# A fused attention and feed-forward kernel: gates on later loads removed, plan times of DMA transposes changed, two more x tiles transposed by TensorE

## The chip, the cores and the metric

The kernel runs on one core of a Trainium2 chip. Its time is the device time of one execution in microseconds (us). Four executions of the kernel before took 213.44 to 215.19 us, with a median of 213.62 us. One execution was recorded by the hardware profiler; it took 213.64 us.

## The reference

The program computes attention and feeds its result to a two-layer network. Cut to what matters (batch 4, 8 heads, 768 positions, head dimension 64; 3072 tokens, model width 512, hidden width 2048):

```python
scores = scale * q @ k.T + bias            # bias: -slope[h] * distance
keep = is_global | is_local                # first 8 positions, or the last 96
scores = where(keep, scores, -1e9)
a = softmax(scores)
x = (a @ v).transpose(0, 2, 1, 3).reshape(3072, 512)
h = x @ w_in
out = (relu(h) ** 2) @ w_out
```

Inputs and output are float32 in DRAM. The kernel computes with bfloat16 operands and sums in float32.

## The kernel before

**Tiles.** The 3072 tokens are 24 tiles of 128 (index `j`, six to a sequence). For the attention of a tile only its own keys and those of the tile to its left matter; the eight global keys are copied into the left tile's columns. The feed-forward part takes two tiles at a time, so there are 12 blocks. Each block has 8 steps of the first product (`s1`, line 689: 8 matmuls of 256 columns into `hT`), each followed by a relu on ScalarE (ACT, line 710), a square on VectorE (DVE, line 722) and one step of the second product (`s2`, line 759: 4 matmuls of 512 columns into `acc`). A finished block is copied from PSUM and stored to DRAM from SyncE's queue (SP, line 794).

**Path of one tile.** GpSimd (POOL) issues three loads that cast to bfloat16, line 200: q and k into a buffer `qk_ring[slot(j)]`, and v into a buffer of its own. Tiles 0 to 5 have a buffer each; tiles from 6 on share three buffers in turn, so load `j` must wait until tile `j-3` has been transposed out of its buffer. q and k are then transposed to `qkT[j % 12]`: for tiles below `JQK = 6` by TensorE through PSUM (`tr`, line 383) with a copy; from tile 6 on by one DMA transpose that SyncE issues (`T`, line 407). Then come the scores (`sc`, line 463), the exponential (line 509), the multiplication by the bias factors (line 534), the product with v (`pv`, line 576) and the normalization (lines 603 and 604), which gives `x` of the tile. `x` is transposed to `xT` for the feed-forward part: for tiles below `JX = 6` by TensorE (`trx`, line 639) with a copy on DVE or ACT (lines 317 and 315); from tile 6 on by a DMA transpose that SyncE issues (line 663).

**Gates.** From tile 8 on, a load has a gate: a memset of the first column of `qk_ring[slot(j)]` on DVE (line 357, 60 ns). It overwrites what the transpose of tile `j-3` reads and is itself overwritten by the load, so the load follows the gate, and the gate follows the transpose. The place of the gate in DVE's order sets the time from which the load may go:

```python
deps=qk_users[slot(j)] + [ld, xT_sp.get(j - 3)], key=base - 9,
```

Here `ld` is the data of load `j-1`, and `xT_sp` holds the DMA transposes of x (only those).

**The planner.** The order of instructions on each engine is written by `Plan`, a list scheduler that runs when the program is built. Each operation has a cost per engine (made-up times such as 0.87 us for an `s1` step), a list of operations that must come before it, and a key. Time after time the planner takes the operation with the smallest start plus 0.01 times its key. While an engine has a choice of work, the start is the same for all, and the key decides. Operations that emit nothing stand for time that passes: `("data", j)` for the landing of a load, `("moved", j)` and `("xmoved", j)` for the landing of a DMA transpose, `("land", ...)` for the first loads. They occupy pretended resources, `DMAQ` or `DMA`. The plan sets order alone; on the chip every instruction waits for the data it needs, and each engine and each queue runs in the order written.

A tile's keys are counted from `base = 8*(j//2) - lead + 4*(j%2)`, with a lead of 12 (10 and 11 for tiles 6 and 7), on the scale on which `s1` step `n` has the key `n` (plus constants by kind of operation, in `SHIFT`). Scores of tile `j` also depend, in the plan, on `s1` step `4*j - 12`. The DMA transpose of tile `j` depends, in the plan, on x of tile `j-3` having been transposed (`xT_op[j - 3]`). `s1` of a block depends on the `xT` of both its tiles.

Of the kernel before, what the change touches and what calls it, by code (L numbers as in the profile page):

```python
# [104 lines left out]
def kernel(  # L105
# [17 lines left out]
    NT = B * TPB  # L123
# [17 lines left out]
    NFIRST = 4  # L141
    NSPLIT = 4
    NBIAS = 3
    JQK, JX = 6, 6
    NQ, NKT = 3, 2 * TPB
    NG = 8 - NACC
    G = ("g", NG)
# [27 lines left out]
    pbt = const([P, 2, P], FP32, "pbt")  # L175
    pbw = const([P, 2, P], FP32, "pbw")
    plan = Plan()
    LEADS = {6: 10, 7: 11}
    NHS = 14
    NWARM = 8  # L180
    NLATE, NO = 2, 4
# [9 lines left out]
    def slot(j):  # L191

        return j if j < NFIRST + 2 else NFIRST + 2 + j % NQ
# [34 lines left out]
    def load_tile(j):  # L228
        load_part(0, j)
        load_part(1, j)  # L230
        load_v(j)
# [81 lines left out]
    def any_copy(e, dst, src):  # L313
        if e == "ACT":
            nc.scalar.copy(dst, src)  # L315
        else:
            nc.vector.tensor_copy(dst, src)
# [25 lines left out]
    for j in range(NT):  # L343
        b, t = divmod(j, TPB)
        first = t == 0
        need = 8 * (j // 2)
        base = need - LEADS.get(j, LEAD) + 4 * (j % 2)


        if j in late:  # L350
            def emit_load(e, j=j):
                load_tile(j)
            gate = None
            if j >= NFIRST + 2 + NQ - 1:

                def emit_gate(e, j=j):
                    nc.vector.memset(qk_ring[slot(j)][:, :, :1], 0.0)  # L357

                gate = plan.op(
                    ("gate", j), {"DVE": 0.07}, emit_gate, deps=qk_users[slot(j)] + [ld, xT_sp.get(j - 3)],  # L360
                    key=base - 9,
                )
            ld = plan.op(
                ("load", j), {"POOLQ": 2.6}, emit_load,
                deps=qk_users[slot(j)] + [ones[j], gate], key=base, ready=issue[0],
            )
            qk_users[slot(j)] = []
            ld = plan.op(("data", j), {"DMAQ": 2.7}, None, deps=[ld])
            land["q", j] = land["k", j] = land["v", j] = ld
# [6 lines left out]
        for n in range(2) if j < JQK else ():  # L376
            users = []

            def emit_tr(e, j=j, n=n, fp=fp):
# [11 lines left out]
                deps=[land["qk"[n], j]], key=base, takes=(*G, [users]),  # L391
            )

            def emit_T(e, j=j, n=n, T_=T_):
                any_copy(e, T_[:, n], tiles.pop(("tr", n, j)))

            c = plan.op(
                ("T", n, j), {"DVE": 0.61 if fp else 0.41, "ACT": 0.48}, emit_T,
                deps=[tr] + ku, key=base + 0.1,
            )  # L400
# [4 lines left out]
        if j >= JQK:  # L405
            def emit_dT(e, j=j, T_=T_):
                nc.sync.dma_start_transpose(
                    out=T_.rearrange("p n a c -> p (n a) c"),
                    in_=qk_ring[slot(j)].rearrange("p n c -> p (n c)"),
                )  # L410

            T = plan.op(
                ("T", j), {"SP": 1.3}, emit_dT,
                deps=[land["q", j], land["k", j], xT_op[j - 3]] + ku, key=base - 6,
            )
            T = plan.op(("moved", j), {"DMAQ": 1.2}, None, deps=[T])
            qk_users[slot(j)].append(T)
            parts = [T]
        kT_users[j % NKT] = ku = []

# [51 lines left out]
        deps = list(parts)  # L472
# [26 lines left out]
        for g in range(groups):  # L499
            for odd in range(2):  # L500
# [26 lines left out]
                def emit_mul(e, j=j, odd=odd, g=g, first=first):  # L527
# [11 lines left out]
                    deps=[x_, maskE0[odd] if first else None],  # L539
# [23 lines left out]
        for hf in range(2):  # L563
# [22 lines left out]
            deps = [mul[0, g], mul[1, g], land["v", j]]  # L586
# [11 lines left out]
            def emit_norm(e, j=j, hf=hf):  # L598
# [14 lines left out]
                deps=[p_] + norm, key=base + 2.3 + 2 * hf,  # L613
# [18 lines left out]
        if j < JX:  # L632
            users = []

            def emit_f(e, j=j):
                trx = ps_g.tile([P, KM, P], BF16, name="trx", tag="g")
                x = tiles["x", j].rearrange("p h d -> p (h d)")
                for kt in range(KM):
                    nc.tensor.transpose(
                        out=trx[:, kt, :], in_=x[:, kt * P : (kt + 1) * P], identity=ident  # L640
                    )
                tiles["trx", j] = trx

            f_ = plan.op(
                ("trx", j), {"PE": 0.24}, emit_f, deps=norm, key=base + 5,
                takes=(*G, [users]),
            )

            def emit_xT(e, j=j, blk=blk, tt=tt):
                if tt == 0:  # L650
                    tiles["xT", blk] = work.tile([P, KM, 2 * P], BF16, name="xT", tag="xT", bufs=3)
                any_copy(
                    e, tiles["xT", blk][:, :, tt * P : (tt + 1) * P], tiles.pop(("trx", j))
                )

            c = plan.op(("xT", j), {"DVE": 0.41, "ACT": 0.48}, emit_xT, deps=[f_], key=base + 5.1, takes=xT_ring)
            users += [f_, c]
            xusers.append(f_)
        else:
            def emit_xT(e, j=j, blk=blk, tt=tt):  # L660
                if tt == 0:
                    tiles["xT", blk] = work.tile([P, KM, 2 * P], BF16, name="xT", tag="xT", bufs=3)
                nc.sync.dma_start_transpose(
                    out=tiles["xT", blk][:, :, tt * P : (tt + 1) * P],
                    in_=tiles["x", j].rearrange("p h d -> p (h d)"),
                )

            c = plan.op(("xT", j), {"SP": 1.2}, emit_xT, deps=norm, key=base + 5, takes=xT_ring)
            xop = xT_sp[j] = c
            c = plan.op(("xmoved", j), {"DMAQ": 0.9}, None, deps=[c])  # L670
            xusers.append(c)
        xT_op[j] = c
        xT_users.append(c)
        xT_of[blk] = xT_users
# [7 lines left out]
    for n, (blk, s) in enumerate(order1):  # L682
        users = []

        def emit_s1(e, blk=blk, s=s):
# [15 lines left out]
            deps=[xT_op[2 * blk], xT_op[2 * blk + 1], land["win", s]],  # L701
# [28 lines left out]
    for o in plan.ops:  # L730
        if o["name"][0] == "sc":
            j = o["name"][1]
# [4 lines left out]
    for blk in range(NBLK):  # L737
# [9 lines left out]
        for s, sub, half in order2:  # L747
# [5 lines left out]
            def emit_s2(e, blk=blk, s=s, sub=sub, half=half, w=w, cols=cols, own=own):  # L753
# [17 lines left out]
                deps=[d, land["wout", s]] + users[-1:],  # L771
# [5 lines left out]
            if s == NSTEP - 1:  # L777
                ousers = []

                def emit_o(e, blk=blk, sub=sub, half=half, cols=cols):  # L780
# [6 lines left out]
                    emit_o, deps=[o], key=8 * blk + s + 1.0, takes=("o", NO, [ousers]),  # L787
# [4 lines left out]
                def emit_st(e, blk=blk, sub=sub, half=half, cols=cols):  # L792
# [9 lines left out]
                    deps=[ev, s1_ops[NLATE, 0] if blk < NLATE - 2 else None],  # L802
# [43 lines left out]
```

## Time and profile before

| What | Value |
|---|---|
| median of four runs | 213.62 us |
| profiled execution | 213.64 us |
| its span, first to last instruction | 211.9 us |
| TensorE matmul busy | 202.4 us (96%) |
| VectorE busy | 138.9 us (66%) |
| ScalarE busy | 119.9 us (57%) |
| GpSimd busy | 73.8 us (35%) |
| mean granted TensorE clock | 1.000 |
| DMA transposes of q and k, of x | 18 and 18 |
| gates on DVE | 16, of 60 ns each |

How to read it: busy time is the union of an engine's instructions, and since matmuls overlap in TensorE's pipeline, a high share alone says little. The page cuts the span into 40 slices and gives a digit for each (9 means 90% or more). A row of the timeline gives start, duration, engine, line, operation and tiles, and in brackets the idle time of the engine before it with what ended it. "SPq" is SyncE's queue of DMA issues; its duration is that of the issue, and the landing of the data is counted apart. "issue" is waiting that the profile explains by nothing else.

### The profile page before, as it was taken

The page shows a single profiled execution, that of the slowest core. Times are in us where ns is not written, and L with a number is a line of the kernel's source. Part 1 is how long each engine was busy: PE and PEld are TensorE (multiplying, and loading weights), DVE is VectorE, ACT ScalarE, POOL GpSimd, SP SyncE. Part 2 cuts the span into 40 slices and gives each one's busy share as a digit, 9 for nine tenths or more (in the row PEclk, how much of TensorE's full clock was granted, in tenths as well). Part 3 has the DMA queues.
Part 4 walks back from the last instruction along what each step waited for, and adds up shares of the span by engine and source line. Part 5 has one row for each costly group of instructions (what it writes and reads, how often), then busy time and mean ns, then how long its engine had stood idle before and what let it go on. Part 6 is the DMA issues. An engine that isn't in the chain of part 4 may idle for free.

```text
span 211.9 us, 4984 instructions
## 1 busy us (share of the span) xinstructions
PE 202.4 (96%) x1946; PEld 140.7 (66%) x1976; DVE 138.9 (66%) x377; ACT 119.9 (57%) x223; POOL 73.8 (35%) x91
## 2 busy tenths in 40 slices
PE   7799999999999999989999999999999999999994
PEld 3576877555766767656666666766667667666773
DVE  7589878623966866656677677575677577564530
ACT  6787668224663763843844854753845754733531
POOL 8996766440224314404404404404134400000000
PEclk9999999999999999999999999999999999999999
DMA  8999999999699999699999599998999894210202
GB/s 122 153 173 186 184 191 198 176 191 149 173 97 97 206 103 125 138 139 103 150 169 95 107 178 99 116 186 96 167 138 101 114 179 83 90 33 3 99 2 99
DMA packets 113703, 27.59 MB, mean 130 GB/s; under 512 B 104336, under 2 KB 110736, under 8 KB 113680
## 3 DMA queue, kind: packets, MB, share of 16 engines
q0 software_dynamic: 79200, 13.37, 82.4%
q1 hardware_dynamic: 34480, 13.90, 32.8%
q8 instruction: 15, 0.25, 0.5%
q14 instruction: 8, 0.07, 0.1%
HBM read 27.26 MB, written 6.29 MB: 158 GB/s over the span
## 4 chain that ended last, share of the span: by engine, by line
PE 82%; DMA 7%; POOL 5%; ACT 2%; issue 2%; DVE 0%; SPq 0%; POOLq 0%; ACTq 0%
PE hT L689 37%; PE acc L759 36%; PE sc L463 4%; PE po L576 4%; DMA win<-in_moe_w_in_dram 4%; DMA qkT<-qk 3%; POOL qk L200 3%; POOL v L200 2%; POOL win L200 1%; ACT esc L509 1%; ACT hr L710 1%; ACT o L315 0%; PE tr L383 0%; DVE hs L722 0%; POOL pbi L254 0%
## 5 line engine op out<-in xcount | busy, mean ns | idle before, releaser
L689 PE MATMUL hT<-xT,win 128*128 128x256 bf16 x768 | 98.4, 273 | 0.7 <-DMA win<-in_moe_w_in_dram 0.3
L710 ACT ACTIVATE hr<-hT 128x512 f32<-128x512 f32 x96 | 57.7, 601 | 72.1 <-PE hT L689 68.4
L759 PE MATMUL acc<-wout,hs 128*128 128x512 bf16 (+1 forms) x370 | 93.3, 370 | 2.0 <-issue 0.8
L689 PEld LDWEIGHTS <-win 128*128 128x128 bf16 x768 | 74.0, 98 | 25.5 <-DMA win<-in_moe_w_in_dram 1.1
L722 DVE TENSOR_TENSOR hs<-hr 128x512 bf16<-128x512 f32 x96 | 65.8, 688 | 32.5 <-ACT hr L710 31.5
L200 POOL DMA_DIRECT2D qk<-in_q_dram x23 | 20.6, 896 | 89.4 <-DVE qk L357 55.3
L759 PEld LDWEIGHTS <-hs 128*128 128x128 bf16 x400 | 35.7, 97 | 23.7
L509 ACT ACTIVATE esc<-sc 128x512 bf16<-128x512 f32 x78 | 43.6, 607 | 4.2 <-PE sc L463 4.0
L534 DVE TENSOR_TENSOR at<-esc,E 128x512 bf16<-128x512 bf16 x78 | 32.2, 422 | 10.9 <-ACT esc L509 9.5
L200 POOL DMA_DIRECT2D v<-in_v_dram x24 | 21.7, 904 | 1.4 <-DMA win<-in_moe_w_in_dram 0.9
L604 DVE TENSOR_TENSOR x<-po,rs 128x256 bf16<-128x256 f32 x48 | 20.4, 424 | 1.7
L200 POOL DMA_DIRECT2D qk<-in_k_dram x23 | 20.4, 887 | 1.0 <-DMA win<-in_moe_w_in_dram 0.9
L576 PEld LDWEIGHTS <-at 128*128 128x128 bf16 x352 | 16.0, 98 | 4.7 <-ACT at L509 0.8
L576 PE MATMUL po<-v,at 128*128 128x65 bf16 x352 | 17.8, 193 | 0.6 <-DMA v<-in_v_dram 0.5
L315 ACT COPY o<-acc 128x512 f32<-128x512 f32 (+1 forms) x21 | 11.2, 568 | 7.6 <-PE acc L759 7.6
L463 PEld LDWEIGHTS <-qkT 64*128 64x128 bf16 x352 | 10.0, 94 | 8.0 <-issue 4.0
L603 DVE RECIPROCAL rs<-po 128x4 f32<-128x4 f32 x48 | 8.7, 181 | 9.3 <-PE po L576 9.2
L463 PE MATMUL sc<-qkT 64*128 64x128 bf16 x192 | 13.4, 219 | 0.8 <-DMA qkT<-qk 0.6
L463 PE MATMUL sc<-qkT,qkT 64*128 64x128 bf16 x160 | 11.5, 216 | 0.0
L200 POOL DMA_DIRECT2D win<-in_moe_w_in_dram x8 | 6.2, 800 | 1.8 <-DMA win<-in_moe_w_in_dram 1.3
L200 POOL DMA_DIRECT2D wout<-in_moe_w_out_dram x8 | 5.7, 718 | 2.0 <-DMA win<-in_moe_w_in_dram 1.2
L550 DVE COPY qkT<-qkT 128x32 bf16<-128x32 bf16 x16 | 3.5, 219 | 4.4 <-PE sc L463 4.4
(41 smaller groups left out, 58.3 us busy)
## 6 DMA issues: line engine op xcount, KB each, us to landing
out_dram<-o SPq DMA_DIRECT2D x23, 256.0 KB, 2.3
v<-in_v_dram POOLq DMA_DIRECT2D x24, 128.0 KB, 5.8
qk<-in_q_dram POOLq DMA_DIRECT2D x23, 128.0 KB, 4.7
qk<-in_k_dram POOLq DMA_DIRECT2D x23, 128.0 KB, 5.2
win<-in_moe_w_in_dram POOLq DMA_DIRECT2D x8, 256.0 KB, 8.2
wout<-in_moe_w_out_dram POOLq DMA_DIRECT2D x8, 256.0 KB, 9.3
qkT<-qk SPq DMA_TRANSPOSE x18, 3.6
xT<-x SPq DMA_TRANSPOSE x18, 3.5
```

Of the source, the lines that this page charges most:

```text
L200: nc.gpsimd.dma_start(out=dst, in_=src)
L315: nc.scalar.copy(dst, src)
L463: nc.tensor.matmul(out=tiles["sc", j, odd, g][:, at, :], lhsT=qkT[(j - kt) % NKT][half, 1, pair, :], rhs=qkT[j % NKT][half, 0, pair, :], s ...
L509: nc.scalar.activation(out=esc, in_=tiles.pop(("sc", j, odd, g)).rearrange("p a c -> p (a c)"), func=Act.Exp, scale=scale,)
L534: nc.vector.tensor_mul(at, tiles.pop(("esc", j, odd, g)), bias)
L576: nc.tensor.matmul(out=po[:, hi, :], lhsT=tiles["at", j, odd, g][:, at * P : (at + 1) * P], rhs=v_sb[kj][:, h, :], start=(i == 0), stop=(i ...
L603: nc.vector.reciprocal(rs, po[:, :, D : D + 1])
L604: nc.vector.tensor_tensor(out=x[:, 4 * hf : 4 * hf + 4, :], in0=po[:, :, :D], in1=rs.to_broadcast([P, 4, D]), op=Alu.mult,)
L689: nc.tensor.matmul(out=hT[:, c, :], lhsT=w_in_sb[s][:, kt, c * P : (c + 1) * P], rhs=tiles["xT", blk][:, kt, :], start=(kt == 0), stop=(kt ...
L710: nc.scalar.activation(hr, tiles.pop(("hT", blk, s)), Act.Relu)
L722: nc.vector.tensor_mul(hs, hr, hr)
L759: nc.tensor.matmul(out=tiles["acc", blk, sub, half], lhsT=hs[:, c, sub * P : (sub + 1) * P], rhs=w_out_sb[s][:, c, cols], start=(s == 0 an ...
```

## The change

Five edits, all in what the planner is given:

- `JX` goes from 6 to 8, so x of tiles 6 and 7 is transposed by TensorE and copied, and no longer by a DMA transpose.
- Tiles 10 to 23 get a lead of 14 where they had 12.
- Tiles 6 to 11 get an operation `("seen", j)` after `("moved", j)`, which emits nothing and takes 1.6 us in the plan. The scores of the tile wait for it in the plan; the release of the buffer does not.
- Tiles 9 and 11 get the like for x, `("xseen", j)`, of 1.5 us.
- Only loads 8, 9 and 10 keep a gate (`JGATE = 11`). Later loads wait for the transpose that frees their buffer and for nothing else.

```diff
-    JQK, JX = 6, 6
+    JQK, JX = 6, 8
...
-    LEADS = {6: 10, 7: 11}
+    LEADS = {6: 10, 7: 11} | {j: 14 for j in range(10, NT)}
+    SAFE = {j: 1.6 for j in range(6, 12)}
+    SAFEX = {9: 1.5, 11: 1.5}
+    JGATE = 11
...
             gate = None
-            if j >= NFIRST + 2 + NQ - 1:
+            if NFIRST + 2 + NQ - 1 <= j < JGATE:
...
             T = plan.op(("moved", j), {"DMAQ": 1.2}, None, deps=[T])
             qk_users[slot(j)].append(T)
+            if j in SAFE:
+
+                T = plan.op(("seen", j), {"DMA": SAFE[j]}, None, deps=[T])
             parts = [T]
...
             c = plan.op(("xmoved", j), {"DMAQ": 0.9}, None, deps=[c])
             xusers.append(c)
+            if j in SAFEX:
+                c = plan.op(("xseen", j), {"DMA": SAFEX[j]}, None, deps=[c])
```

## The prediction

> **What bounds the kernel.** I read the page's slices and busy times first, then stretches of the span, then who waits for whom on TensorE, then the transposes and the queues that carry them.
>
> ```profile
> PE   7799999999999999989999999999999999999994
> PEclk9999999999999999999999999999999999999999
> DMA  8999999999699999699999599998999894210202
> ```
>
> TensorE (PE) is full in nearly every slice at full granted clock; so are the DMA engines until slice 34. Either could be the bound. The answer by stretches (columns: window, its length, then busy time and instructions of PE, weight loads, DVE, ACT, POOL) tells which:
>
> ```profile
> 22.00:43.00 21.00, 20.84 (x214) 15.55 (x215) 16.34 (x37) 12.89 (x24) 12.80 (x16) 1.00 1.66 187
> 43.00:64.00 21.00, 20.64 (x187) 13.15 (x189) 12.46 (x32) 10.42 (x20) 5.27 (x6) 1.00 1.33 150
> 64.00:85.00 21.00, 20.84 (x211) 14.57 (x214) 14.84 (x41) 10.66 (x20) 7.89 (x9) 1.00 1.32 136
> 85.00:100.00 15.00, 14.12 (x126) 9.56 (x123) 9.31 (x23) 8.51 (x16) 5.27 (x6) 1.00 1.06 125
> 100.00:203.00 103.00, 101.63 (x952) 70.80 (x969) 67.73 (x166) 59.07 (x108) 23.68 (x27) 1.00 0.97 114
> ```
>
> From 22 to 203 us PE is busy 20.84 + 20.64 + 20.84 + 14.12 + 101.63 = 178.07 of 181.00 us. The idle 2.93 us is all that any change to loads and transposes in this stretch can give back. Before 22 us the first weights arrive (tiles 0 to 5, which the diff leaves alone); after 203 us PE runs the last 40 second-product matmuls without a stop. The waits of PE in that stretch:
>
> ```profile
> PE acc L759 <- issue: 0.8, 5, 0.2
> PE sc L463 <- DMA qkT<-qk: 0.6, 1, 0.6
> PE acc L759 <- DVE qkT L550: 0.2, 1, 0.2
> ```
>
> One wait on a DMA, 0.6 us, once. The "issue" rows are short turns around score matmuls, which stay. Where the 0.6 us is, the timelines of SyncE and GpSimd show:
>
> ```profile
> 86.41 1.14 SPq L794 DMA_DIRECT2D out_dram<-o  x2
> 87.66 1.29 SPq L407 DMA_TRANSPOSE qkT<-qk  x1
> 91.74 1.19 SPq L663 DMA_TRANSPOSE xT<-x  x1
> ...
> 86.98 0.88 POOL L200 DMA_DIRECT2D qk<-in_q_dram  x1 [4.62 <-DVE qk L357]
> 87.85 0.88 POOL L200 DMA_DIRECT2D qk<-in_k_dram  x1
> 88.72 0.90 POOL L200 DMA_DIRECT2D v<-in_v_dram  x1
> ...
> 93.82 0.40 PE L463 MATMUL sc<-qkT 64*128 64x128 bf16 x8 [0.62 <-DMA qkT<-qk]
> ```
>
> The q/k transpose of tile 12 starts at 87.66, in the middle of two stores and the load of tile 13, and lands at 93.77, 6.1 us later; scores 12 start at 93.82. The landing times of the two kinds of transposes (qkT, then xT; minimum, median, maximum):
>
> ```profile
> DMA to landing us min/median/max: 3.0/3.6/6.8
> DMA to landing us min/median/max: 2.4/3.5/7.0
> ```
>
> So a transpose costs 2.4 to 3.1 us in clear queues and up to 7.0 in full ones. I paired each with its consumer's first weight load. Slack is tiny in half of the places: scores 12, 14, 16, 18 and 22 start 0.04, 0.31, 0.31, 0.31 and 0.29 us after their transpose lands; feed-forward blocks 3, 4, 7 and 8 start 0.10, 0.11, 0.04 and 0.21 us after their second xT. The old order sits on an edge, but pays only about 0.9 us there: 0.62 at scores 12 and 0.28 of weight-load wait at 129.32.
>
> **The change, part by part.**
>
> *x of tiles 6 and 7 by TensorE.* Two DMA transposes (2 x 1.19 us of SyncE) go; 8 transposes and two copies come. The rows for tiles 0 to 5:
>
> ```profile
> L639 PE MATMUL trx<-ident,x x24: 219/219/229, 11.7 to 41.9; 128*128 128x128 bf16 x24
> L317 DVE COPY xT<-trx x2: 405/415/425, 12.3 to 42.1; 128x512 bf16<-128x512 bf16 x2
> ```
>
> 219 ns is the time of one by itself; they overlap, and the group of four at 41.71 takes 0.39 us in the timeline, which is 219 + 3 x 56 ns. So 8 x 0.056 = 0.45 us of PE, all on the bound. The copies (0.42 us on DVE, or 0.59 on ACT by the row for ACT) lie beside PE: DVE is busy 12.46 of 21 us in 43 to 64. Were that cover gone, block 3 would start up to 0.6 us later. In exchange its x no longer waits for the 5.95 us transpose issued at 59.37, landed at 65.31, which made the plan fill with second-product matmuls until 65.42. Filling loses no PE time, so this earns at most 0.1 us. Bounds of this part: 0 to +0.6; I take +0.45.
>
> The Trainium skill, "TensorE: Matmul & The Clock Gate", Part 4, gives some 275 ns per 128x128 transpose in a kernel and speaks against this edit: by its figure 8 x 0.275 = 2.2 us, an estimate, and the sum would be some 1.75 us higher. The pitch of 56 ns in this trace decides against it.
>
> *Gates.* DVE loses 13 memsets of 60 ns (tiles 11 to 23): 0.8 us, off the path. More important is what they held: each load of tile j waited for its gate's place in DVE's order, 9 to 16 us after the transpose of tile j-3 freed its buffer (transpose 10 landed at 74.29, load 13 went at 86.98). Now GpSimd waits for that landing itself; nothing else is behind it but later loads. Gates 9 and 10 also lose their tie to x transposes of tiles 6 and 7 (`xT_sp` has none), so load 9 could go at about 53, when load 8 has landed (52.51), not at 56.92, and the later ones follow. From load 11 on a load can come that much earlier. Its q/k transpose can go right after the x transpose of tile j-3 instead of behind the load. Scores 12 then have microseconds of slack: minus 0.62.
>
> What it may cost: loads 10 to 13 now come nearly back to back, and transposes fly among them. The dearest transposes seen are 6.8 and 7.0 us, against 3.6 in the median. Bounds for a transpose in the new crowd: 2.4 to 7.0 us; I take 4.7, which transposes 16, 18 and 22 took, each started 0.16 us behind a load.
>
> The Trainium skill, "DMA: Bandwidth & Descriptors", Rules for kernel authors, says that a transpose next to ordinary DMAs needs nothing; that is about correct data. In time this trace disagrees (3.0 against 4.7 to 6.8 us). By that rule the old gates protected nothing and the crowd is free.
>
> *Two steps more lead for tiles 10 to 23.* Scores of tile j now follow first-product step 4j-10 (scores 12 come after step 38); by the keys they can follow step 4j-12, where the code's own dependency stands. A step lasts (192.72 - 97.22) / 48 = 1.99 us, so scores, norms and x transposes come up to 4.0 us earlier against the blocks that read them. That covers the 0.28 at 129.32 and another 3 us of lateness. The work is the same: 0 by itself.
>
> *Extra time in the plan for transposes 6 to 11 and x 9 and 11.* No instruction; it moves consumers back in PE's order where the plan expected the data too early, up to 1.6 us in plan, with other matmuls ahead of them. 0 as long as the second product has a backlog; if not, up to 1.6 us once.
>
> **Sum**, against the profiled execution (213.64 us: span 211.9 and 1.74 around it; the median of the runs is 213.62, the same): 213.64 - 0.62 - 0.28 + 0.45 = 213.2 us.
>
> **Rivals.**
>
> *The lead asks for data that are not there (214.2).* Scores 10 would move from 76.94 to 72.9, but transpose 10 started at 71.20. If its load comes no earlier than now (k landed at 69.90), a crowded transpose lands at 74.6 to 76.7. The added plan time should order other work there; an error of about 1 us remains, and x of tile 9, with 0.11 us of slack and no new lead, may land in 7.0 instead of 5.66 us: 1.2 us. One of them: about 1 us, 213.2 + 1.0 = 214.2. For it: slack was zero there before. Against: the stretch is short.
>
> *Slower: odd x transposes run into free loads, block after block (216.9).* The gate is what kept loads off certain transposes. If each x transpose of tiles 11, 13, ... 21 took the worst 7.0 us, the lateness beyond today's slack would be 1.5, 2.4, 2.0, 2.2, 2.4 and 2.2 us (today's landings 3.4, 2.4, 5.0, 4.6, 3.2 and 3.3; slacks 2.1, 2.2, 0.0, 0.2, 1.4 and 1.5). A lead gained of 2.4 us or more swallows it; at 1.5 us the losses are 0 + 0.9 + 0.5 + 0.7 + 0.9 + 0.7 = 3.7: 216.9. So it decides where less than 2.4 of the 4.0 us arrive. For it: with DMA busy, x transposes 12 and 7 took 7.0 and 5.95 beside loads. Against: a load now starts when a q/k transpose lands, some 5 us after an x transpose, and should be over before the next one 6 to 10 us later.
>
> *Much faster (211.2).* All 2.93 us of idle time vanish: 213.64 - 2.93 + 0.45. Against: most of it is turns at score matmuls, which stay.
>
> **Chances and range.** Forecast 213.2: 0.58. The early lead, 214.2: 0.20. Crowded x transposes, 216.9 (215.5 to 220): 0.18. Much faster: 0.04. About 1% (2.1 us) is what a measurement of this kernel can tell from no change; the first two lie within it, so faster 0.04, same 0.78, slower 0.18. Range: from 212.4 (half of the remaining idle time gone too) to 216.5, which leaves out 0.04 and some 0.12 of the slower case.
>
> **What would show it.** In the changed profile: PE's waits on qkT gone from 85 us on; landings of qkT with slack of 4 us or more; GpSimd's waits on DVE gone after load 10, replaced by waits on qkT; 32 trx matmuls; PE busy about 0.45 us more; median landing of both transposes above 3.6. Wrong would be: PE waiting for xT at block starts 5 to 10, or PE idle above 2.9 us between 22 and 203.

## The result and the profile after

The changed kernel takes 212.78 us (median of 34 executions, 212.23 to 214.54), the kernel before 214.37 us (median of 55, 212.84 to 218.19). The ratio is 0.9939, with a 95% interval of 0.9925 to 0.9954: about 1.3 us or 0.6% faster. Medians here are of all executions; ratios and their intervals leave out those more than 1.5% above the fastest of their kernel. The change also narrows the spread: in two later sets of runs, with 12 executions each, it stayed between 212.38 and 214.00, while the kernel before beside it went from 212.86 to 219.09.

The profiled execution took 213.1 us with a span of 211.3. The slices of TensorE, its clock and the DMA engines after:

```profile
PE   7999999999999989999999999999999999999993
PEclk9999999999999999999999999999999999999999
DMA  9999999999999999999999999999943121120202
```

The DMA digits now fall at slice 30, not 34: the loads are over about four slices earlier. By stretches (window, length, then busy time and instructions of PE, weight loads, DVE, ACT, POOL):

```profile
22.00:43.00 21.00, 20.84 (x212) 15.23 (x213) 16.09 (x36) 12.76 (x24) 11.91 (x15) 1.00 1.66 187
43.00:64.00 21.00, 20.84 (x179) 12.87 (x181) 11.36 (x31) 10.69 (x21) 10.53 (x12) 1.00 1.60 168
64.00:85.00 21.00, 20.07 (x218) 14.49 (x220) 15.58 (x39) 11.88 (x24) 9.46 (x11) 1.00 1.62 143
85.00:100.00 15.00, 14.73 (x143) 10.14 (x145) 11.17 (x26) 9.07 (x18) 3.69 (x5) 1.00 1.58 159
100.00:203.00 103.00, 101.62 (x934) 70.84 (x951) 69.27 (x156) 54.48 (x101) 18.41 (x21) 1.00 0.81 101
```

GpSimd's work (the last busy column) moves forward: 10.53 us in 43 to 64, where it was 5.27. The waits of TensorE from 22 to 203 us:

```profile
PE acc L767 <- issue: 0.6, 4, 0.2
PE sc L469 <- DMA qkT<-qk: 0.6, 1, 0.6
PE acc L767 <- DVE qkT L556: 0.3, 2, 0.2
```

The wait on qkT is no longer at scores 12. The transpose of tile 12 now starts 10.7 us earlier (it was 87.66), and its scores come when they are due:

```profile
76.93 1.25 SPq L410 DMA_TRANSPOSE qkT<-qk  x1
...
89.22 0.39 PE L469 MATMUL sc<-qkT 64*128 64x128 bf16 x7
```

It has moved to scores 10. The timelines of GpSimd, SyncE and TensorE there:

```profile
56.89 0.88 POOL L203 DMA_DIRECT2D qk<-in_q_dram  x1 [0.40 <-issue]
60.94 0.88 POOL L203 DMA_DIRECT2D qk<-in_q_dram  x1 [1.42 <-DVE qk L360]
...
68.90 5.91 SPq L410 DMA_TRANSPOSE qkT<-qk  x2
...
77.37 0.23 PE L469 MATMUL sc<-qkT 64*128 64x128 bf16 x2 [0.61 <-DMA qkT<-qk]
```

The load at 56.89 is that of tile 11, and the one at 60.94, which still waits for a gate, that of tile 10: the planner put the ungated load ahead of the gated one. Both transposes start at 68.90 and 70.74 in a full queue, and number 10 takes 8.4 us. All landings of transposes after (q/k, then x):

```profile
DMA to landing us min/median/max: 3.1/5.6/8.4
DMA to landing us min/median/max: 2.4/3.4/6.7
```

So a q/k transpose became 2 us dearer in the median (3.6 to 5.6), and from scores 11 on it does not matter, because there is slack enough (3.17 us or more). Slack is the time from the landing of a transpose to its consumer's first weight load, paired as in the prediction:

| Consumer | slack before, us | slack after, us |
|---|---|---|
| scores 9, 10 | 0.14, 2.66 | 4.38, 0.04 |
| scores 12, 14, 16, 18, 22 | 0.04, 0.31, 0.31, 0.31, 0.29 | 8.19, 5.02, 10.28, 10.57, 13.05 |
| scores 13, 15, 17 | 3.85, 4.70, 3.36 | 3.17, 9.12, 12.26 |
| feed-forward block 4 | 0.11 | 2.92 |
| blocks 5, 6, 7, 8 | 2.10, 2.18, 0.04, 0.21 | 1.53, 4.90, 4.62, 2.93 |

Scores of tile j follow first-product step 4j-12 from tile 11 on (step 36 for tile 12, 40 for 13, 44 for 14), as the lead of 14 lets them (steps are counted from 0). What holds the loads now is the transpose that frees their buffer, with the gates left over for loads 8 to 10 alone (GpSimd's waits after):

```profile
POOL qk L203 <- DMA qkT<-qk: 52.2, 10, 9.9
POOL qk L203 <- DVE qk L360: 13.2, 3, 6.8
```

**Two profiles with every record.** Both profiles above lack some 30 of TensorE's matmuls (1946 and 1953 in the page's first part, where 1976 and 1984 were issued). Later profiles of the same two kernels have them all. The stretch from 22 to 203 us, before and after:

```profile
22.00:203.00 181.00, 180.01 (x1706) 123.29 (x1705) 120.90 (x297) 102.06 (x187) 54.46 (x64) 1.00 1.15 130
```

```profile
22.00:203.00 181.00, 181.00 (x1712) 123.81 (x1711) 123.77 (x287) 99.33 (x184) 53.93 (x63) 1.00 1.18 129
```

In that execution of the changed kernel TensorE is busy for 181.00 of 181.00 us. In that of the kernel before the 0.99 us that is missing is exactly two waits on transposes, at scores 12 and at block 3:

```profile
PE sc L463 <- DMA qkT<-qk: 0.7, 1, 0.7
PE hT L689 <- DMA xT<-x: 0.3, 1, 0.3
```

No "issue" rows are left in either. By this comparison some two of the 2.93 us that the first profile called idle were matmuls that had not been recorded.

### The profile page after: what moved, and what is told of

Read it like the earlier page. It is cut to its first block, busy times and chain, and to the rows that moved or that the text cites. A ratio compares the mean times of both kernels' runs of the same rounds, so it can differ in the third digit from the quotient of the medians.

```text
span 211.3 us, 4968 instructions
## 1 busy us (share of the span) xinstructions
PE 202.8 (96%) x1953; PEld 141.3 (67%) x1984; DVE 142.5 (67%) x368; ACT 117.5 (56%) x221; POOL 73.8 (35%) x91
## 4 chain that ended last, share of the span: by engine, by line
PE 80%; DMA 8%; POOL 7%; issue 1%; ACT 1%; DVE 0%; SPq 0%; POOLq 0%
PE acc L767 37%; PE hT L697 34%; PE sc L469 4%; PE po L582 4%; DMA qkT<-qk 4%; DMA win<-in_moe_w_in_dram 4%; POOL qk L203 4%; POOL v L203 2%; POOL win L203 1%; ACT hr L718 1%; PE trx L645 0%; DVE hs L730 0%; POOL wout L203 0%; ACT esc L515 0%; ACT o L318 0%
## 5 line engine op out<-in xcount | busy, mean ns | idle before, releaser
L515 ACT ACTIVATE esc<-sc 128x512 bf16<-128x512 f32 x78 | 41.3, 610 | 1.9 <-PE sc L469 1.3
L318 ACT COPY o<-acc 128x512 f32<-128x512 f32 (+1 forms) x17 | 9.3, 564 | 8.1 <-PE acc L767 7.6
L556 DVE COPY qkT<-qkT 128x32 bf16<-128x32 bf16 x16 | 4.1, 257 | 9.7 <-PE sc L469 9.7
L320 DVE COPY o<-acc 128x512 f32<-128x512 f32 x8 | 5.5, 692 | 1.7 <-PE acc L767 1.6
```

What stands on the lines that cost most here:

```text
L515: nc.scalar.activation(out=esc, in_=tiles.pop(("sc", j, odd, g)).rearrange("p a c -> p (a c)"), func=Act.Exp, scale=scale,)
```

## The experiments

Theory 1: TensorE is full, and the change pays because late transposes find slack, which takes free loads and the lead together. Rivals: the gain is x of tiles 6 and 7 alone (theory 2); it is the early q/k transposes alone (theory 3); it is luck at the start of the execution. Kernels of one set ran on one chip and share runs of the kernel before, so each is read against the kernel before of its own set. The first four rows are one set, the next four another, the last four a third. `less_free` has 6 executions, `before_again` 10, all others 12.

| Kernel | median (range), us | before in its set | ratio, 95% interval | TensorE's waits on qkT + xT in its profile, us |
|---|---|---|---|---|
| less_x67 | 217.39 (213.09 to 219.97) | 215.31 | 0.9952, 0.9898 to 1.0005 | 1.2 + 0 |
| less_lead | 214.18 (212.94 to 216.78) | 215.31 | 0.9958, 0.9925 to 0.9991 | 0 + 0.5 |
| less_free | 219.10 (216.30 to 221.48) | 215.31 | 1.0127, 1.0042 to 1.0212 | 3.7 + 0 |
| less_safe | 214.74 (212.90 to 216.20) | 215.31 | 0.9968, 0.9930 to 1.0006 | 0 + 0 |
| after_again | 213.02 (212.59 to 214.00) | 214.94 | 0.9919, 0.9883 to 0.9956 | 0 + 0 |
| before_again | 214.47 (212.75 to 216.81) | 214.94 | 0.9941, 0.9890 to 0.9992 | 0.7 + 0.3 |
| only_free | 217.09 (215.25 to 220.18) | 214.94 | 1.0085, 1.0046 to 1.0124 | 0.5 + 2.3 |
| only_x67 | 213.90 (213.00 to 215.79) | 214.94 | 0.9989, 0.9956 to 1.0023 | 1.3 + 0.2 |
| after_third | 212.90 (212.38 to 213.69) | 214.45 | 0.9941, 0.9910 to 0.9972 | 0 + 0 |
| after_dup17 | 212.56 (212.46 to 213.57) | 214.45 | 0.9939, 0.9910 to 0.9967 | 0 + 0 |
| untied | 215.97 (213.72 to 217.75) | 214.45 | 1.0051, 1.0006 to 1.0095 | 0 + 1.7 |
| gate10 | 213.12 (212.45 to 214.13) | 214.45 | 0.9948, 0.9913 to 0.9983 | 0 + 0 |

### How far to trust a ratio: the two kernels again

The kernel before, unchanged (`before_again`), and the changed kernel (`after_again`, `after_third`).

> The kernel before, unchanged, for a second profile. Ratio 1.00 within 0.4%. Theory 1 (with slack below 0.35 us at scores 12, 14, 16, 18, 22 and blocks 3, 4, 7, 8, the wobble of landing times becomes waits, different ones in each execution): waits of TensorE for qkT and xT of 0.5 to 3 us in all, not only at scores 12. Rival (the order of before is fixed and its waits are as in the first profile): 0.6 us at scores 12 alone.

> The changed kernel once more, beside the others of this call, and a second profile of it. Theory 1 (its gain is that late transposes find slack): median 0.5 to 0.9% below the kernel before on the same chip, and again less spread; in the profile no wait of TensorE for qkT or xT after 85 us, and any wait before that only at scores 10. Rival (the gain is a lucky start-up): the waits after 85 us look like those of before.

> The changed kernel a third time, as the yardstick of this call: 0.5 to 0.9% below the kernel before, waits of TensorE on DMA between 22 and 203 us at scores 10 or nowhere, 0 to 0.7 us.

The kernel before against itself gave 0.9941, with an interval that leaves out 1.00, where 1.00 within 0.4% was expected. So within one set a difference of 0.6% is not proof of anything; less_lead, less_safe and less_x67 lie inside that band. The changed kernel's own ratios, 0.9919 to 0.9941, are hardly further from 1. The evidence for it is that its median lies 1.5 to 1.9 us below that of the kernel before in each of three sets, that its highest execution of the last two sets (214.00) is below the median of the kernel before, and that its fastest, 212.23 us, is 0.5 us below the fastest of the kernel before, 212.75. Its waits on transposes are as expected: none in `after_again` and `after_third`, 0.6 us at scores 10 in the first profile. A wait of 0.28 us on weights at block 1 in `after_third` was not expected.

The second profile of the kernel before waits at scores 12 again, and at block 3, where it had not waited in the first. Scores 9, 14, 16, 18 and 22 and blocks 7 and 8 start 0.04 to 0.31 us after their data there too. So theory 1's wobble was seen, but small: 0.62 and 0.99 us, against an expectation of 0.5 to 3.

### Taking parts away

Each of these four is the changed kernel with one part undone.

Without the early loads: gates on all loads again, the lead kept.

```diff
-    JGATE = 11
+    JGATE = NT
```

> The changed kernel with the gates on all loads from tile 8. Theory 1 (slack): loads and q/k transposes land late again, so scores cannot use the lead, and slack at scores 12, 14, 16 is below 0.5 us again: 213.5 to 214.4 us. Rival (the lead alone is the gain): 212.8.

Worse than expected: 1.3% slower than the kernel before, whose gates are the same but for the tie of gates 9 and 10 to the DMA transposes of x 6 and 7. The lead asks for scores two steps sooner, and the transposes come no sooner: waits at scores 13, 16 and 20 of 0.36, 1.2 and 2.1 us. And the longest of them costs more than itself. The stretches around it in this kernel's profile (after the POOL column comes the granted clock of TensorE):

```profile
158.00:160.50 2.50, 0.36 (x4) 0.01 (x2) 0.69 (x1) 0.56 (x1) 0.00 (x0) 1.00 2.05 161
160.50:162.00 1.50, 1.50 (x22) 1.10 (x23) 0.60 (x2) 1.07 (x3) 0.00 (x0) 0.93 0.66 97
162.00:164.00 2.00, 2.00 (x9) 1.06 (x7) 1.29 (x4) 1.59 (x4) 1.21 (x2) 0.50 0.68 130
164.00:166.00 2.00, 1.91 (x16) 1.24 (x16) 0.68 (x3) 0.00 (x0) 1.42 (x2) 0.70 1.16 74
```

```profile
160.50 0.23 PE L469 MATMUL sc<-qkT 64*128 64x128 bf16 x2 [2.13 <-DMA qkT<-qk]
```

After 2.13 us of waiting the clock falls to half, for (0.07 x 1.5 + 0.5 x 2.0 + 0.3 x 2.0) / 0.5 = 3.4 us, in which 1.7 us of work is lost. The wait at scores 20 cost 3.8 us, not 2.1. The Trainium skill, "TensorE: Matmul & The Clock Gate", Part 1, has the halved clock and a window of about 3.4 us, which agrees; it asks for a whole idle window, and here 2.13 us was enough.

Waits of 1.2 to 1.74 us in other places and profiles of this study left the clock at 1.00. One drop does not show that the length alone decides. In the trace the halved stretch runs from 161.79 to 165.21, 3.41 us, and other stretches of unchanged clock are whole multiples of that (208.21 us in the first profile of the kernel before, 61 times 3.413). Counted back in such steps, the wait of 2.13 us lies with 2.1 us in one step, while the 1.74 us of `untied`, further down, is split into 0.90 and 0.84 us. No run here separates length from place.

Without the lead, the loads free:

```diff
-    LEADS = {6: 10, 7: 11} | {j: 14 for j in range(10, NT)}
+    LEADS = {6: 10, 7: 11}
```

> The changed kernel with the lead of tiles 10 to 23 back at 12. Theory 1 (slack): the q/k transposes stay early, but blocks 5 to 10 start close behind their x transposes again, now in fuller queues: waits of TensorE for xT of 0.3 to 1.5 us in all, 213.2 to 214.3 us. Theory 3 (the early q/k transposes are the whole gain): 212.8, no different from the changed kernel.

In the profile the q/k transposes keep their slack (5.2 us or more at scores 11 to 23), while block 7 waits 0.5 us for x of tile 15, 6.5 us after its issue, and block 6 has 0.40 us of slack:

```profile
129.76 0.50 PE L697 MATMUL hT<-xT,win 128*128 128x256 bf16 x3 [0.50 <-DMA xT<-x]
```

The waits are as theory 1 says; the ratio cannot be told from that of the changed kernel or, by the repeat of the kernel before, from 1.

Without the extra plan time for transposes 6 to 11:

```diff
-    SAFE = {j: 1.6 for j in range(6, 12)}
-    SAFEX = {9: 1.5, 11: 1.5}
+    SAFE = {}
+    SAFEX = {}
```

> The changed kernel without the extra plan time for transposes 6 to 11 and x 9 and 11. Theory 1: TensorE reaches scores 8 to 11 or blocks 4 and 5 before their data, once or twice, 0.5 to 1.5 us in all: 213.3 to 214.3 us. Rival (plan time that emits nothing is worth nothing): 212.8.

Not settled. Its profile, at 213.03 us, shows no wait on a transpose; scores 10 had 0.16 us to spare, scores 6 and 7 had 0.60 and 0.95. Its median lies 0.6 us below the kernel before, where the changed kernel lies 1.5 to 1.9 below in other sets, but no run of the changed kernel stood beside it.

Without x of tiles 6 and 7 by TensorE:

```diff
-    JQK, JX = 6, 8
+    JQK, JX = 6, 6
```

> The changed kernel with x of tiles 6 and 7 by DMA transpose again (JX = 6). Theory 1 (slack: the gain comes from free loads and the lead, and x of 6 and 7 by TensorE costs 0.45 us): 0.4 us faster than the changed kernel, 212.4 us where the changed one has 212.8 and the one before 214.4. Theory 2 (x of 6 and 7 by TensorE is the gain, since block 3 no longer waits for a transpose of 6 us): back to about 214.4.

Theory 1's 0.4 us of gain did not come. The profile, of an execution of 213.73 us, waits 0.29 us at scores 10 and 0.92 us at scores 12. Four of the 12 executions took 213.09 to 214.37 us, and the ratio of 0.9952 counts these alone; the other eight took 216.52 to 219.97 us, and none of them was profiled. What these two transposes do is therefore read from the next kernels.

### One part alone

The kernel before with x of tiles 6 and 7 by TensorE (`only_x67`), and the kernel before with gates on loads 8 to 10 alone (`only_free`):

```diff
-    JQK, JX = 6, 6
+    JQK, JX = 6, 8
```

```diff
+    JGATE = 11
...
-            if j >= NFIRST + 2 + NQ - 1:
+            if NFIRST + 2 + NQ - 1 <= j < JGATE:
```

> The kernel before with x of tiles 6 and 7 by TensorE and nothing else changed. Theory 1: eight more transposes on a full TensorE, 0.45 us or 0.2% slower, since blocks 4 on are as they were. Theory 2 (this edit is what pays, by way of loads 9 and 10, whose gates it sets free, or of block 3): 0.3% faster or more.

> The kernel before with gates on loads 8 to 10 alone and nothing else changed. Theory 1 (free loads take the q/k transposes off the edge, x transposes stay on it and meet fuller queues): slack of the q/k transposes of 4 us and more from tile 13 on, waits for xT at blocks 7 and 8; 0.2 to 0.6% below the kernel before. Rival (the crowd costs what the early loads bring): no difference or slower.

`only_x67` is level with the kernel before (0.9989): neither the 0.2% of theory 1 nor the gain of theory 2. Its transposes 8 to 11 have 2.9 to 5.3 us of slack where they had 0.1 to 3.1, and its waits moved to scores 14 (1.32 us), which the edit does not touch directly.

`only_free` is slower by 0.85%, where 0.2 to 0.6% faster was expected. Its waits:

```profile
PE hT L697 <- DMA xT<-x: 2.3, 2, 1.3
PE sc L469 <- DMA qkT<-qk: 0.5, 2, 0.4
```

The q/k transposes gained what was foreseen (4.5 to 15 us of slack from tile 13 on). But x transposes kept their old places behind the norms, and now meet free loads. At block 7, GpSimd's, SyncE's and TensorE's rows:

```profile
122.20 0.88 POOL L203 DMA_DIRECT2D qk<-in_q_dram  x1 [2.49 <-DMA qkT<-qk]
123.06 0.89 POOL L203 DMA_DIRECT2D qk<-in_k_dram  x1
...
124.33 1.20 SPq L669 DMA_TRANSPOSE xT<-x  x1
...
131.71 1.05 PE L697 MATMUL hT<-xT,win 128*128 128x256 bf16 x8 [1.29 <-DMA xT<-x]
```

A load starts at 122.20, x of tile 15 goes at 124.33 while it moves, lands at 131.66 (7.3 us later), and TensorE, which has nothing else ahead of block 7 in its order, waits 1.29 us. The other wait is at block 3, for x of tile 7, issued at 59.31 and landed at 66.48, 7.2 us later:

```profile
66.62 1.03 PE L697 MATMUL hT<-xT,win 128*128 128x256 bf16 x8 [1.04 <-DMA xT<-x]
```

Theory 3 falls with this kernel: its q/k transposes are early, and it is slower. So free loads by themselves are harmful, and so is the lead without them (`less_free`). That free loads need the lead above all is not shown: `less_lead` has them with x of 6 and 7 by TensorE and the added plan time, but no lead; it waits 0.5 us at block 7, and its ratio is 0.9958.

### What x of tiles 6 and 7 does

The gates of loads 9 and 10 are tied, in the plan, to the DMA transposes of x 6 and 7. `JX = 8` takes both away. The kernel `untied` takes the tie alone: JX is 6, and

```diff
-                    deps=qk_users[slot(j)] + [ld, xT_sp.get(j - 3)],
+                    deps=qk_users[slot(j)] + [ld, xT_sp.get(j - 3) if j > 10 else None],
```

> The changed kernel with x of tiles 6 and 7 by DMA transpose (JX = 6), but gates 9 and 10 not tied to those two transposes. If the good of TensorE's transposes was only that loads 9 and 10 were set free: as fast as the changed kernel or 0.45 us faster, with little spread. If it was the two DMA transposes themselves, their places in SyncE's queue and in the full DMA queues: waits at scores 9, 10 or 12 or at blocks 3 and 4 of 0.5 to 1.5 us and a wide spread, like the kernel of the changed one without this edit.

It is 0.5% slower than the kernel before, and its order of loads on GpSimd is that of the changed kernel. SyncE's, GpSimd's and TensorE's rows at block 3:

```profile
61.67 1.81 SPq L669 DMA_TRANSPOSE xT<-x  x1
...
61.75 0.88 POOL L203 DMA_DIRECT2D qk<-in_q_dram  x1 [1.41 <-DVE qk L360]
62.62 0.89 POOL L203 DMA_DIRECT2D qk<-in_k_dram  x1
...
68.15 1.91 PE L697 MATMUL hT<-xT,win 128*128 128x256 bf16 x16 [1.74 <-DMA xT<-x]
```

The transpose of x 7 goes together with load 10 and lands at 68.01, 6.3 us later; block 3 waits 1.74 us. `only_free` waits at the same place. So the good of the edit is not that loads 9 and 10 are set free; by these two profiles it is that x of 7 stays out of queues that the earlier loads have filled. Of the places named beforehand block 3 waited, and longer than the 0.5 to 1.5 us foreseen; scores 9 to 12 and block 4 did not.

### Slack itself: a load made late

```diff
-        load_part(0, j)
+        for _ in range(2 if j == 17 else 1):
+            load_part(0, j)
```

> The changed kernel with the q load of tile 17 issued twice, the second after the first has landed, so that k and q of this tile and every later load come some 5 us later. Theory 1 (slack): transposes 17 to 21 had 6 to 15 us to spare, so nothing waits and the time is that of the changed kernel, within 0.3 us. Rival (the pace of the loads bounds this stretch): 3 to 5 us longer.

The q load of tile 17, its copy, and the loads behind it:

```profile
99.42 0.88 POOL L203 DMA_DIRECT2D qk<-in_q_dram  x1 [3.10 <-DMA qkT<-qk]
104.45 0.88 POOL L203 DMA_DIRECT2D qk<-in_q_dram  x1 [4.15 <-DMA qk<-in_q_dram]
105.32 0.88 POOL L203 DMA_DIRECT2D qk<-in_k_dram  x1
...
107.05 0.90 POOL L203 DMA_DIRECT2D qk<-in_q_dram  x1
```

The k load goes at 105.32, where `after_third` beside it had it at 100.83: 4.5 us later, and load 18 follows at 107.05 instead of 102.61. The transpose of tile 17 is issued at 111.07 (111.39 in `after_third`), so its place in SyncE's order, and not the load, set its start. It lands at 119.07 instead of 115.77, 3.3 us later (the k load landed at 110.19, before the issue), and its scores still have 9.6 us. TensorE waits for no transpose, and the median, 212.56 us, is 0.34 us below that of `after_third`, 212.90. A delay of 4.5 us of the loads costs nothing in this stretch.

### A try at the last wait

```diff
-    JGATE = 11
+    JGATE = 10
```

> The changed kernel with gates on loads 8 and 9 alone (JGATE = 10). In the changed kernel load 11 has no gate and is issued ahead of load 10, which has one, so transpose 10 lands 0.04 to 0.35 us before scores 10. Without gate 10, load 10 goes first: slack at scores 10 of 3 us or more, no wait there, and 0.2 to 0.6 us less than the changed kernel beside it. Rival (the queue stays as full, another of transposes 9 to 13 takes the lateness): no difference, or a wait of 0.5 us or more at another score or block.

The step worked and paid nothing. Scores 10 have 5.70 us of slack instead of 0.33, and block 4 has 0.93 instead of 3.18. The median is 213.12 us, against 212.90 for the changed kernel beside it. In the profiles there was nothing to win: `after_third` already waited for no transpose.

## Why the prediction was right

Predicted were 213.2 us, from 213.64, and a range of 212.4 to 216.5; measured were 212.78, against 214.37. Direction and range held, and the size was three times the forecast: 0.6%, not 0.2%. That the time came so near is partly luck: the base was an execution 0.73 us below the median, and several terms, as told below, were wrong by themselves.

- **TensorE is the bound.** Right, and more so than the prediction knew: 181.00 of 181.00 us busy in a profile with every record. The upper bound on any gain, 2.93 us of idle time, was wrong: it counted unrecorded matmuls, and so did the "issue" rows that were taken for turns at score matmuls. The true idle time in the profiled executions of the kernel before is about 1 us.
- **Minus 0.62 at scores 12, minus 0.28 at block 7.** The first was right: it is gone, with 8.2 us of slack. The second was no cost. The weight load waited, but no idle time stands before the matmuls of block 7:

```profile
128.94 0.59 PE L759 MATMUL acc<-wout,hs 128*128 128x512 bf16 x2
129.32 0.81 PEld L689 LDWEIGHTS <-win 128*128 128x128 bf16 x8 [0.28 <-DMA xT<-x]
129.38 1.04 PE L689 MATMUL hT<-xT,win 128*128 128x256 bf16 x8
```

Matmuls of 512 columns follow each other every 0.22 us here (four take 1.03 us at 127.84, the last by itself 0.38), and 128.94 + 2 x 0.22 = 129.38: block 7 was not late.

- **Plus 0.45 for eight transposes.** The price held: the new transposes, at 61.48 and 64.55 of the first profile after, take 0.40 and 0.39 us for four, and the paragraph on the mis-sized term below finds about 0.47 us of added work. What failed is the other half of that step, "this earns at most 0.1 us". With x of 6 and 7 left to DMA transposes and the gates untied, block 3 waits 1.74 us for x of tile 7 in the queues that the same change fills (`untied`).
- **Free loads, "scores 12 then have microseconds of slack: minus 0.62".** Failed as a term of its own: alone they cost 0.85% (`only_free`). The slower rival, odd x transposes running into free loads, shows there: 7.3 us for x 15, close to the 7.0 assumed. With x of 6 and 7 by TensorE and the plan time it is smaller without the lead (6.5 us and a wait of 0.5 us in `less_lead`).
- **The lead, "the work is the same: 0 by itself".** Failed as well: with the gates kept it costs 1.3% (`less_free`), through waits and a halved clock that the prediction had not priced. The parts do not add up by themselves; each was priced as if the others were there.
- **The rival of scores 10.** It came true in one profile of three, with 0.61 us, for a reason that the prediction had missed: load 11 without a gate overtakes load 10 with one.
- **Plan time for transposes 6 to 11, "0 as long as the second product has a backlog".** Neither shown nor refuted.
- **The signs.** Of those that the prediction named, two did not come: scores 10 and 13 have 0.04 and 3.17 us of slack, not 4 or more, and the median landing of x transposes is 3.4 us, not above 3.6.

**The mis-sized term** is the old waits: 0.90 us in the sum, read from one execution of 213.64 us where the median of 55 is 214.37. TensorE in fact waited 0.62 us for transposes in that execution and 0.99 us in `before_again`. From the first matmul of block 1 to the end, which leaves the start-up out, these two took 185.50 and 186.01 us, the three profiled executions after 186.07 (with 0.61 us of waiting at scores 10), 185.42 and 185.38. Less these waits that is 184.88 and 185.02 before, 185.46, 185.42 and 185.38 after. So the work grew by about 0.47 us, as priced, and 0.6 to 1.0 us of waits went, with one of 0.61 us coming in one profile of three. The gain is 0.14 us in the mean, 0.36 us without that profile, against the forecast of 0.44.

The same stretch took 185.38 us in `after_dup17`, 185.37 in `gate10`, 185.49 in `less_safe`, 186.18 in `less_lead`, 186.31 in `less_x67`, 186.73 in `untied`, 187.18 in `only_x67`, 188.33 in `only_free` and 191.73 in `less_free`. These are single executions, but free of the start-up, and they follow TensorE's waits in the table above, roughly. Leaving out the lead, x of 6 and 7 by TensorE or the free loads thus costs 0.8, 0.9 and 6.3 us against the 185.4 of the changed kernel without a wait. As one of the three executions of the changed kernel took 186.07, only the last of these stands clear of the spread.

Most of the 1.6 us between the medians is not in this stretch of these profiles. The start-up differs more: block 1 starts at 26.37 and 27.29 before and at 25.23, 25.40 and 25.63 after, though the orders of TensorE, GpSimd and SyncE up to there are the same. A first k load (tile 0's, which SyncE issues) landed at 6.39 and 6.64 before, and at 5.22, 5.29 and 6.10 after. Over all 14 profiles block 1 starts at 25.23 to 27.29, and at 26.76 in `less_lead`, so luck at the start can move one execution by as much as the gain. That it moves the medians is neither shown nor excluded.

The other open cause is executions of the kernel before in which more of its ten tight places wait than in the two profiled. It fits the wider spread, and the mean granted clock on record for each execution points the same way. One halved stretch costs 1.7 us, about 0.008 of the time, and the profile of `less_free` with one such stretch has a mean of 0.990. Means of 0.992 or less stand in 16 of 109 executions of the kernel before, 1 of 59 of the changed one, 7 of 12 of `less_x67` and 6 of 12 of `untied`. But none of these was profiled, so which waits dropped the clock there is not known.

## What to carry to other kernels

When one engine is full, a change to transfers is worth what that engine waits for, and how near the other transfers are to making it wait: pair each transfer with its consumer, write down the slack, and treat a row of slacks below 0.3 us as a possible cost that one profile may not show. Parts of such a change should be priced together: here free loads alone were slower by 0.85%, the change without free loads by 1.3%, and the change without the lead was 0.8 us longer in one profile, with a ratio that could not be told from that of the whole. A transfer that must cross the crowd was better moved to another path (`untied`). Before calling an engine's gaps idle time, compare its instruction count with the program's.

## What was not expected of the hardware

A single wait of TensorE of 2.13 us in a full stream was followed by half the granted clock for 3.4 us (0.50 in the stretch from 162 to 164 us of `less_free`), so that the wait cost 3.8 us in all; waits of 1.2 to 1.74 us in the profiles were not. And fuller queues did no harm where there was slack: the median q/k transpose took 3.6 us in the first profile before and 6.0 us in `after_again`, one there reached 11.1 us (tile 16), and TensorE waited for none of them.
